# Loading a block an iteration before it is split, and two more weight tiles prepared ahead, in a fused attention and gated-MLP kernel

## The chip, the cores and the metric

The kernel runs on one core of one Trainium2 chip. The core has five engines with queues of their own: TensorE (PE, with its weight loads shown apart as PEld), VectorE (DVE), ScalarE (ACT), GpSimd (POOL) and SyncE (SP). SP and ACT also issue DMA transfers, which 16 DMA engines carry out. The metric is the device time of one execution in microseconds (us). Before the change the median of three runs is 1359.01 us (1357.99 to 1361.42).

## The reference

Linear attention over 8 batches, 8 heads, 576 positions and a head size of 64, and then a gated MLP on the 4608 tokens that come out, 512 wide, with 1536 hidden columns:

```python
def phi(x):
    proj = einsum('bhsd,df->bhsf', x, w_phi)             # 64 -> 128
    proj = proj - max(abs(proj), axis=-1, keepdims=True)
    return concatenate([exp(proj), exp(-proj)], -1)       # 256 features
q_p, k_p = phi(q), phi(k)
num = einsum('bhsf,bhfd->bhsd', q_p, einsum('bhsf,bhsd->bhfd', k_p, v))
den = einsum('bhsf,bhf->bhs', q_p, sum(k_p, axis=2)) + 1e-6
x = (num / den)                                           # to [4608, 512]
xn = x / sqrt(mean(x * x) + 1e-6) * rms_g
gate, val = xn @ w_gate, xn @ w_val                       # 512 -> 1536
out = (gate * sigmoid(gate) * val) @ w_out                # 1536 -> 512
```

## The kernel before

Every product is done at fp32 accuracy with a two-part form: an operand is split into a high part (a cast on ACT) and a low part (a subtraction on DVE or POOL), and three matmuls (high by high, low by high, high by low) stand for one. The helper that does a split is `_split`; its cast shows in the profile at L60 and its subtraction at L61. The moe weights arrive as 64-bit numbers, are decoded to fp32 by pieces and stored to DRAM (wgs, wvs, wos), to be loaded again where they are used.

There are three stages.

**Attention.** 8 batches with 4 pairs of heads give 32 pairs. A loop over `i` runs four parts of the work, front, mid, back and last, on four consecutive pairs, and merges their instructions into one stream. When the four pairs of a batch are done, the batch's x, transposed, lies in the DRAM tile xs. Whatever part of x is complete is used at once. Tokens come in 12 blocks of 384 (NB, T). Of the 12 column tiles of the hidden layer (128 columns each, NJ), the first three (J1) are computed during attention, from x that isn't normalised yet, because the norm is a factor for each token that can be multiplied in later. This work is called a fill. For each block a fill loads x (L461), splits it into xo (L60 and L61), and runs six units: three column tiles for gate (fg) and value (fv), 12 matmuls each (L476). Each result is copied on ACT from PSUM to a tile fo (L479, two buffers) and stored to gvs (L480). The weights of the fills, the pool wfp, stay in SBUF until the end of the next stage. The list `fills` holds load, split and units of the blocks that are complete, and from the moment it has more than 16 entries (RES) 2.5 entries are taken in each iteration. Two fills that need the last batch, for the blocks 10 and 11, are kept back (tail).

**Stage G** runs over the 12 blocks and, in each, over the nine other column tiles j (JN). `prep` loads a block's x (L141), sums its squares (ACT and POOL, then two matmuls with a matrix of ones), normalises x on DVE and splits it, with the low part on POOL. gv (L556) does 24 matmuls for a block and a j: gate to PSUM fp, value to gp. hidden applies Silu on ACT (L541), multiplies on DVE (L543) and stores h to hs in DRAM (L544). gv_raw loads the stored gvs of one of the first three column tiles (L563), multiplies the norm in and does the same. The gate and value weights come with block 0, by load_gv, which loads wc from ACT's own DMA queue (L536) and splits it to wg and wv. The two tail fills follow gv at block 0, j = 8 and block 1, j = 4.

**The output stage** multiplies hs by w_out for 18 groups (gi) of 256 tokens, with a Strassen-Winograd form of seven products in place of eight (L717, 18 matmuls each). Its weights are six pairs of tiles, wh and wl for kp = 0 to 5, made by load_o (L576): four transfers wc (L582), four subtractions on DVE (L583), two splits. Two of the six are made during stage G (PRE), four at the start of the output stage. A group's hidden values are loaded to a tile ht by hload (L688); from it, DVE makes the sums st (L652 to L660), and five operands are split with the low part on POOL, two (a11, a12) on DVE. hload for a group is written two groups ahead.

The order of the instructions on an engine isn't that of the program text. The Tile framework places them by a simulated timeline, an instruction where its operands and its buffer are ready by that simulation. Within an engine or queue the order is then fixed: an instruction that waits holds all behind it. Buffers of closed pools are given to new pools, and whoever takes one waits for its last user.

## Time and profile before

| | |
|---|---|
| median of three runs | 1359.01 us |
| the profiled execution's own time | 1366.07 us |
| its span on the core | 1364.3 us |
| mean granted TensorE clock | 0.977 of full |
| PE busy | 1303.9 us, 9108 matmuls |
| DVE, ACT, POOL busy | 878.0, 716.1, 610.6 us |
| HBM read, written | 126.04 MB, 69.50 MB |

In the profiled execution attention runs up to about 580 us, stage G from there to 1071 us, the output stage to the end. The lines below come from several views. A line of a timeline has the start (us from the span's beginning), the duration, engine, line, operation, tiles and count, and in brackets the idle time of that engine just before and what ended it. SPq and ACTq are the DMA issues of SP and ACT. A line of the waits says who waited for whom, the total, the number of times and the longest. A line of the groups has the busy time, the mean of one in ns, the idle time before and its releasers. "Granted clock" is the share of the full TensorE clock that was granted in a stretch.

### The profile page before, as it was taken

The numbers are of one execution on the slowest core, as the hardware profiler recorded it, in microseconds if no ns is written. First come the engines' busy times: TensorE is split into PE (matmuls) and PEld (weight loads), VectorE is DVE, ScalarE is ACT, GpSimd is POOL, SyncE is SP. The second block draws the span as 40 slices with busy tenths as digits, with TensorE's granted clock in tenths as the row PEclk, the third lists the DMA queues.
The fourth block names the chain that finished last, engine by engine and source line by source line (L and its number), as shares of the span: only waits on it lengthen the run. The fifth ranks groups of instructions, "written<-read, shape, count | busy, mean of one in ns | idle before, by whom it ended". The sixth has DMA issues, their size and how long they took to land.

```text
span 1364.3 us, 24782 instructions
## 1 busy us (share of the span) xinstructions
PE 1303.9 (96%) x9108; PEld 1291.0 (95%) x9108; DVE 878.0 (64%) x1293; ACT 716.1 (52%) x1490; POOL 610.6 (45%) x580
## 2 busy tenths in 40 slices
PE   7988989999999999989999999999999699999998
PEld 7888989999999999879999999999999699999998
DVE  6897857676778676453246665555542788787673
ACT  5986767776768676643333444333431344444441
POOL 3764635454646345501023333223311357776773
PEclk9997989998999999989999999999999899999999
DMA  5554555556545653475454544544433324534531
GB/s 153 129 141 113 151 166 151 156 152 181 172 144 156 174 158 112 140 216 156 150 180 159 170 130 159 156 148 131 132 125 109 99 97 144 166 125 147 159 128 48
DMA packets 198953, 197.18 MB, mean 145 GB/s; under 512 B 69104, under 2 KB 180848, under 8 KB 198832
## 3 DMA queue, kind: packets, MB, share of 16 engines
q1 hardware_dynamic: 189328, 190.88, 46.3%
q10 hardware_dynamic: 9504, 4.72, 1.2%
q8 instruction: 72, 1.18, 0.4%
q14 instruction: 49, 0.40, 0.1%
HBM read 126.04 MB, written 69.50 MB: 143 GB/s over the span
## 4 chain that ended last, share of the span: by engine, by line
PE 84%; DMA 5%; DVE 5%; ACT 2%; issue 2%; SPq 1%; ACTq 0%; POOL 0%; DVEq 0%
PE fp L556 16%; PE gp L556 16%; PE fp L476 8%; PE acc L346 7%; PE gz L717 5%; PE gd L717 5%; PE gy L717 5%; PE sm L410 3%; PE fp L717 3%; PE fp L410 3%; PE pp L306 2%; PE sm L293 2%; PE pp L308 2%; PE sm L359 2%; PE pp L307 2%
## 5 line engine op out<-in xcount | busy, mean ns | idle before, releaser
L375 POOL TENSOR_TENSOR ql<-eq,qh 128x256 fp32r<-128x256 f32 x256 | 218.8, 886 | 86.7 <-issue 50.2
L556 PE MATMUL fp<-xo,wg 128*128 128x384 f32 x1296 | 244.1, 336 | 6.4 <-ACT sl L541 6.4
L556 PE MATMUL gp<-xo,wv 128*128 128x384 f32 x1296 | 242.9, 335 | 0.0
L556 PEld LDWEIGHTS fp<-xo,wg 128*128 128x128 f32 x1296 | 228.1, 189 | 7.0 <-ACT sl L541 6.8
L556 PEld LDWEIGHTS gp<-xo,wv 128*128 128x128 f32 x1296 | 227.1, 188 | 0.0
L543 DVE TENSOR_TENSOR h<-sl,gp 128x384 f32<-128x384 f32 x108 | 59.6, 552 | 159.8 <-PE gp L556 112.1
L310 DVE TENSOR_REDUCE mx<-pp 128x4 f32<-128x512 f32 (+1 forms) x160 | 101.1, 633 | 69.4 <-PE pp L308 68.3
L541 ACT ACTIVATE sl<-fp 128x384 f32<-128x384 f32 x108 | 52.6, 488 | 177.2 <-PE fp L556 172.7
L346 PE MATMUL acc<-vm,ek 128*128 128x65 f32 x1024 | 134.8, 272 | 1.9 <-ACT ek L333 1.9
L346 PEld LDWEIGHTS acc<-vm,ek 128*128 128x128 f32 x1024 | 131.1, 197 | 2.2 <-ACT ek L333 2.2
L54 POOL TENSOR_TENSOR wa<-raw,wa 128x192 f32<-128x192 f32 (+1 forms) x112 | 62.4, 578 | 156.9 <-issue 85.4
L61 POOL TENSOR_TENSOR xo<-x,xo 128x768 fp32r<-128x768 f32 x24 | 52.3, 2202 | 160.1 <-ACT xo L60 160.1
L371 ACT ACTIVATE qh<-sm 128x512 fp32r<-128x512 f32 (+1 forms) x192 | 96.9, 505 | 0.0
L306 PE MATMUL pp<-wh,th 128*128 128x256 f32 x288 | 89.3, 310 | 6.4 <-ACT th L60 4.3
L476 PE MATMUL fp<-xo,fg 128*128 128x384 f32 x432 | 92.3, 348 | 1.9 <-ACT xo L60 1.8
L370 ACT ACTIVATE eq<-sm 128x512 f32<-128x512 f32 x128 | 78.3, 612 | 14.8 <-PE sm L359 14.0
L61 POOL TENSOR_TENSOR s2l<-st,s2h 128x768 fp32r<-128x768 f32 x18 | 35.0, 1947 | 112.7 <-ACT s2h L60 110.0
L308 PE MATMUL pp<-wh,tl 128*128 128x256 f32 x288 | 83.5, 298 | 0.0
L476 PE MATMUL fp<-xo,fv 128*128 128x384 f32 x360 | 80.6, 353 | 2.3 <-ACT fo L479 2.3
L307 PE MATMUL pp<-wl,th 128*128 128x256 f32 x288 | 82.3, 286 | 0.0
L377 POOL TENSOR_TENSOR ql<-eqr,qh 128x256 fp32r<-128x256 f32 x32 | 24.5, 765 | 124.9 <-ACT qh L371 119.5
L476 PEld LDWEIGHTS fp<-xo,fg 128*128 128x128 f32 x432 | 76.0, 192 | 2.9 <-ACT xo L60 2.1
(192 smaller groups left out, 3535.6 us busy)
## 6 DMA issues: line engine op xcount, KB each, us to landing
hs<-h SPq DMA_DIRECT2D x144, 192.0 KB
ht<-hs SPq DMA_DIRECT2D x18, 1536.0 KB
x<-xs SPq DMA_DIRECT2D x24, 768.0 KB
gvs<-fo SPq DMA_DIRECT2D x72, 192.0 KB
gvr<-gvs SPq DMA_DIRECT2D x36, 384.0 KB
rc<-di SPq DMA_DIRECT2D x32, 288.0 KB
kt<-in_k_dram SPq DMA_DIRECT2D x32, 256.0 KB
qt<-in_q_dram SPq DMA_DIRECT2D x32, 256.0 KB
```

The source lines that it names most:

```text
L61: (lo_eng or nc.vector).tensor_tensor(lo, x, hi.bitcast(F32), ALU.subtract)
L306: nc.tensor.matmul(o, th[:, cs], wh, start=True, stop=False)
L307: nc.tensor.matmul(o, th[:, cs], wl, start=False, stop=False)
L308: nc.tensor.matmul(o, tl[:, cs], wh, start=False, stop=True)
L310: nc.vector.tensor_reduce(mx[:, 0:2 * m], pp[:, 0:2 * m], axis=AX.X, op=ALU.max, apply_absolute_value=True)
L346: nc.tensor.matmul(acc[:, sg, h], e[h][:, sg, j], vm[:, h, j], start=False, stop=(h == 1 and j == T0 - 1))
L371: nc.scalar.activation(hi[:, sg], yi, AF.Exp, scale=1.0 - 2.0 * sg)
L375: nc.gpsimd.tensor_tensor(lo[:, sg, cs], ei[:, sg, cs], hi[:, sg, cs].bitcast(F32), ALU.subtract)
L410: nc.tensor.matmul(o[:, 0:SH], a[:, h, sg], e[:, sg, h, cs], start=(i == 0), stop=(i == 5))
L476: nc.tensor.matmul(fp, w, xx[x][:, c], start=(i == 0), stop=(i == 3 * NC - 1))
L556: nc.tensor.matmul(gp[:, 0:T], w, e[:, c], start=(i == 0), stop=(i == 3 * NC - 1))
L717: nc.tensor.matmul(place[n], a[:, kp], w[:, o], start=(first and kp == 0 and i == 0), stop=(kp == KP - 1 and i == 2), skip_group_check=True)
```

## The change

Loading x becomes a function of its own (fetch), called for fills by `load_x()` at the end of an iteration and followed by the split in a later iteration (`landed()`), so that the load stands one iteration ahead. The list of fills now holds block numbers, the list units only the matmul units; six of them are held back where 16 entries (units, loads and splits) were. The prep of block 0 goes into the same list three iterations earlier. fo has three buffers, which it shares with a small tile of prep. In stage G the loads for prep and for the tail fills stand some j ahead of their use as well, the second tail fill follows j = 6 of block 1 instead of j = 4, and gv_raw and the decoding change places.

The pool of the fill weights lies on the right side of SBUF and is closed after the last tail fill. Its place goes to the pool rg, which now holds four pairs of output weights (PRE = 4) made during stage G instead of two. With this the pools of the output stage are put in another order: the tiles that are there at the seam lie over others of stage G than before.

```diff
-    wfp = x_ctx.enter_context(tc.tile_pool(name="wfp", bufs=1))
+    wf_ctx = ExitStack()
+    wfp = wf_ctx.enter_context(tc.tile_pool(name="wfp", bufs=1, side="right"))
...
-    def prep(bk, pool, name):
-        bs = slice(bk * T, (bk + 1) * T)
+    def fetch(bk):
         x = xip.tile([128, NC, T], F32, name="x")
-        nc.sync.dma_start(out=x, in_=xsv[:, :, bs])
+        nc.sync.dma_start(out=x, in_=xsv[:, :, bk * T:(bk + 1) * T])
+        return x
+
+    def halves(x, lo_eng=None):
+        xhl = xop.tile([128, 2, NC, T], F32R, name="xo")
+        for c in range(0, NC, 2):
+            _split(nc, *(a[:, c:c + 2] for a in (xhl[:, 0], xhl[:, 1], x)), lo_eng=lo_eng)
+        return xhl[:, 0], xhl[:, 1]
+
+    def prep(x, pool, name):
...
-        sl = xm.tile([128, T], F32R, name="sl2", bufs=1)
+        sl = xm.tile([128, T], F32R, name="fo", bufs=3)
...
-                    (tail.append if b == B - 1 else fills.extend)(fill(blocks.pop(0)))
+                    (tail if b == B - 1 else fills).append(blocks.pop(0))
...
-            o = xm.tile([128, T], F32, name="fo", bufs=2)
+            o = xm.tile([128, T], F32, name="fo", bufs=3)
...
-    RES = 2 * (J1 * 2 + 2)
+    RES = J1 * 2
+    units, here = [], []
     dq = quota = 0.0
+    xb = {}
+
+    def load_x():
+        if fills and not here:
+            bk = fills.pop(0)
+            here.append((bk, fetch(bk or 0)))
+
+    def landed():
+        if here:
+            bk, x = here.pop(0)
+            if bk is None:
+                xb[0] = prep(x, ps_f, "fp")
+            else:
+                units.extend(fill(bk, *halves(x)))
...
-        if i == PR - 3:
-            nxt = prep(0, ps_f, "fp")
-        if len(fills) > RES:
-            quota += (NB - 2) * (J1 * 2 + 2) / PR
+
+        if i == PR - 6:
+            fills.insert(0, None)
+        if len(units) <= 3:
+            landed()
+        if len(units) + (len(fills) + len(here)) * J1 * 2 > RES:
+            quota += (NB - 2) * J1 * 2 / (PR - 5)
             nf = int(quota)
             quota -= nf
-            fl, fills[:] = fills[:nf], fills[nf:]
-            _merge([fl])
+            now, units[:] = units[:nf], units[nf:]
+            _merge([now])
+        load_x()
...
-    PRE = 2
+    PRE = 4
...
+            if j == 0 and bk + 1 < NB:
+                xn = fetch(bk + 1)
+            if bk + 1 < NB and j == (2 if bk == 1 else JN // 2):
+                xb[bk + 1] = prep(xn, ps_g, "gp")
+            if bk < 2 and j == (JN // 2, 2)[bk]:
+                xf = fetch(tail[0])
+            if bk < 2 and j == (JN - 1, 6)[bk]:
+                _merge([fill(tail.pop(0), *halves(xf))])
+                if not tail:
+                    wf_ctx.close()
+                    rg = ctx.enter_context(tc.tile_pool(name="rg", bufs=1, reuse_waits="tile", side="right"))
+            if j % (JN // J1) == 0:
                 gv_raw(bk, j // (JN // J1))
...
-    ohp = pool("ohp", bufs=2)
+    ohp = [pool("oh0")]
+    xof = pool("xof")
     ost = pool("ost", bufs=2)
-    xof = pool("xof")
-    xos = pool("xos")
-    xol = pool("xol")
-    xops = dict(a11=xof, a12=xof, s2=xof, s3=xof, s4=xol, a22=xol, s1=xos)
+    ohp.append(pool("oh1"))
+    ow = pool("ow", bufs=2)
     owc = pool("owc", bufs=2)
     owp = pool("owp")
-    ow = pool("ow", bufs=2)
+    xol = pool("xol")
+    xops = dict(a11=xof, a12=xof, s2=xol, s3=xol, s1=xol, s4=xol, a22=xol)
```

Three places show how the instructions move. A row has the line, the operation, the output tile, the inputs and the shape; numbers after a name tell its instances apart.

The first is SP's queue near the third block's load for a fill, at about 184 us of the profile before; x_3894 before is x_2936 after. Before:

```order
L236 DMA wgs_60<-wa_2541 128x384
L273 DMA rb_2917<-in_k_dram 128x1x64
L480 DMA gvs_58<-fo_2631 128x384
L480 DMA gvs_58<-fo_2647 128x384
L441 DMA xs_57<-nd_2195 128x576
L421 DMA di_2422<-dr_2420 128x9
L268 DMA kt_2913<-in_k_dram 128x2x256
L273 DMA rb_2917<-in_q_dram 128x1x64
L461 DMA x_3894<-xs_57 128x4x384
```

After:

```order
L424 DMA dr_2454<-dd_2455 128x9
L141 DMA x_2936<-xs_57 128x4x384
L37 DMA raw_2819<-in_moe_w_val_dram 128x768
L476 DMA gvs_58<-fo_2665 128x384
L476 DMA gvs_58<-fo_2681 128x384
L242 DMA wgs_60<-wa_2575 128x384
L274 DMA kt_2938<-in_k_dram 128x2x256
L279 DMA rb_2942<-in_k_dram 128x1x64
L279 DMA rb_2942<-in_q_dram 128x1x64
```

The load has moved ahead of the two gvs stores, the wgs store, kt and rb.

The second is ACT at the seam from attention to stage G, where the last copies of fo stand between loads (L536, after: L555) and casts of the first gate and value weights. Before:

```order
L479 COPY fo_8118<-fp_8105 128x384
L536 DMA wc_8245<-wgs_60 128x4x128
L536 DMA wc_8245<-wvs_61 128x4x128
L536 DMA wc_8291<-wgs_60 128x4x128
L479 COPY fo_8134<-fp_8121 128x384
L536 DMA wc_8291<-wvs_61 128x4x128
L60 CAST wg0_2_8172<-wc_8245 128x512
L60 CAST wv0_2_8174<-wc_8245 128x512
L60 CAST wg0_3_8176<-wc_8291 128x512
L60 CAST wv0_3_8178<-wc_8291 128x512
```

After:

```order
L475 COPY fo_8118<-fp_8105 128x384
L555 DMA wc_8290<-wgs_60 128x4x128
L555 DMA wc_8290<-wvs_61 128x4x128
L60 CAST wg0_2_8169<-wc_8252 128x512
L60 CAST wv0_2_8171<-wc_8252 128x512
L60 CAST wg0_3_8173<-wc_8290 128x512
L60 CAST wv0_3_8175<-wc_8290 128x512
L555 DMA wc_8328<-wgs_60 128x4x128
L475 COPY fo_8134<-fp_8121 128x384
L555 DMA wc_8328<-wvs_61 128x4x128
```

The last copy, fo_8134, has moved behind the second half of the wc load that it stood ahead of, the four casts, and the first half of the next load.

The third is SP's queue at the seam from stage G to the output stage (hs from h is a store of hidden values, ht from hs the load of a group, wc from wos a piece of output weights). Before:

```order
L544 DMA hs_59<-h_12767 128x384
L544 DMA hs_59<-h_12798 128x384
L582 DMA wc_12853<-wos_62 128x256 x4
L582 DMA wc_12869<-wos_62 128x256 x4
L688 DMA ht_13111<-hs_59 128x12x256
L582 DMA wc_12885<-wos_62 128x256 x4
L681 DMA out_0_dram<-ro_12943 128x512 x2
```

After:

```order
L563 DMA hs_59<-h_12800 128x384
L601 DMA wc_12869<-wos_62 128x256 x2
L563 DMA hs_59<-h_12831 128x384
L601 DMA wc_12869<-wos_62 128x256 x2
L713 DMA ht_12901<-hs_59 128x12x256
L713 DMA ht_12903<-hs_59 128x12x256
L601 DMA wc_12885<-wos_62 128x256 x4
L713 DMA ht_13111<-hs_59 128x12x256
L706 DMA out_0_dram<-ro_12943 128x512 x2
```

Of the weight pieces here, those of the kernel before that are left are the pairs 4 and 5 (wc_12869 and wc_12885). The loads ht_12901 and ht_12903 of the first two groups, which stood some 220 rows further up, in the middle of stage G, now stand here, behind the last store of hidden values.

More of the change, by code (lines that the diff above doesn't have):

```diff
@@ L454, with fill @@
     blocks = list(range(NB))
-    def fill(bk):
-        xx = {}
-        def fetch():
-            xx["x"] = xip.tile([128, NC, T], F32, name="x")
-            nc.sync.dma_start(out=xx["x"], in_=xsv[:, :, bk * T:(bk + 1) * T])
-        def split():
-            xhl = xop.tile([128, 2, NC, T], F32R, name="xo")
-            xx["h"], xx["l"] = xhl[:, 0], xhl[:, 1]
-            for c in range(0, NC, 2):
-                _split(nc, *(a[:, c:c + 2] for a in (xx["h"], xx["l"], xx["x"])))
+    def fill(bk, xh, xl):
+        xx = dict(h=xh, l=xl)
         def unit(j, wi):
```

24 lines of the change are left out of this document (9 added, 15 removed).

## The prediction

> **What bounds the kernel now.** I read the page's busy shares and chain first, then the busy time by stretches, then the waits and timelines around each stretch in which TensorE (PE) is not full.
>
> ```profile
> PE 1303.9 (96%) x9108; PEld 1291.0 (95%) x9108; DVE 878.0 (64%) x1293; ACT 716.1 (52%) x1490; POOL 610.6 (45%) x580
> DVE  6897857676778676453246665555542788787673
> PE 84%; DMA 5%; DVE 5%; ACT 2%; issue 2%; SPq 1%; ACTq 0%; POOL 0%; DVEq 0%
> ```
>
> PE is busy for 1303.9 us of a span of 1364.3 us, and it is 84% of the chain that ended last (DVE's row is its busy tenths in 40 slices of the span). The change issues the same matmuls, so it can only touch the 60.4 us in which PE idles and the time in which PE runs at less than its full clock after such idling. Both show in the stretches (columns: window, length, then busy us and instructions of PE, weight load, DVE, ACT, POOL, then granted clock, DMA share, GB/s):
>
> ```profile
> 190.00:200.00 10.00, 6.38 (x25) 6.09 (x26) 4.21 (x6) 8.60 (x23) 3.58 (x5) 0.66 0.33 85
> 320.00:330.00 10.00, 8.08 (x48) 7.74 (x48) 6.21 (x9) 7.00 (x17) 2.25 (x3) 0.78 0.36 123
> 470.00:480.00 10.00, 7.66 (x45) 7.54 (x46) 7.13 (x12) 9.04 (x21) 4.21 (x7) 0.83 0.41 113
> 580.00:600.00 20.00, 13.55 (x67) 13.04 (x67) 8.22 (x14) 7.60 (x13) 0.00 (x0) 0.84 0.85 239
> 1070.00:1080.00 10.00, 5.60 (x25) 4.58 (x24) 8.58 (x6) 6.67 (x9) 6.23 (x3) 0.82 0.23 74
> 1080.00:1100.00 20.00, 12.29 (x58) 10.50 (x57) 17.92 (x22) 6.33 (x8) 5.00 (x3) 0.66 0.42 131
> 1100.00:1120.00 20.00, 20.00 (x172) 20.00 (x171) 16.63 (x15) 9.17 (x14) 14.21 (x7) 1.00 0.31 103
> ```
>
> I price a stall as the idle time plus busy time times (1 − clock). At 190 to 200 us that is 3.6 + 6.4 × 0.34 = 5.8 us. The two seams are the dear ones: 580 to 600 us costs 6.4 + 13.55 × 0.16 = 8.6 us, and 1070 to 1100 us costs 12.1 + 1.0 + 4.2 = 17.3 us.
>
> **Part 1: x fetched an iteration ahead (attention stage).** The four longest waits of an ACT cast for a fill's x, with other work of ACT queued behind:
>
> ```profile
> 108.96 1.57 ACT L60 CAST xo<-x 128x768 fp32r<-128x768 f32 x2 [3.59 <-DMA x<-xs]
> 191.40 1.56 ACT L60 CAST xo<-x 128x768 fp32r<-128x768 f32 x2 [5.97 <-DMA x<-xs]
> 322.90 1.56 ACT L60 CAST xo<-x 128x768 fp32r<-128x768 f32 x2 [4.87 <-DMA x<-xs]
> 470.32 1.56 ACT L60 CAST xo<-x 128x768 fp32r<-128x768 f32 x2 [5.08 <-DMA x<-xs]
> 193.50 0.58 PE L306 MATMUL pp<-wh,th 128*128 128x256 f32 x1 [4.07 <-ACT th L60]
> 325.05 1.55 PE L346 MATMUL acc<-vm,ek 128*128 128x65 f32 x8 [1.92 <-ACT ek L333]
> 472.34 1.11 PE L359 MATMUL sm<-ident,yq 128*128 128x128 f32 x4 [2.61 <-ACT nd L412]
> 183.91 0.41 SPq L461 DMA_DIRECT2D x<-xs  x1
> ```
>
> The second x was issued at 183.91 and its cast began at 191.40, so a fetch takes about 7.5 us from issue to use; the casts that PE waited for (th, ek, nd) stand behind xo on ACT. If every such stall went, it would be worth, with the rows above, 5.8 (at 190), 1.9 + 8.08 × 0.22 = 3.7 (at 320) and 2.3 + 7.66 × 0.17 = 3.6 us (at 470). But the new order does not remove them all. Up to about 158 us the two programs have the same order on each engine, so the first stall stays. For the second (third block's x), the load now stands ahead of six others (two gvs stores, the wgs store, kt and two rb) that stood ahead of it before, and three more ACT instructions separate it from its cast: I take that stall as gone, −5 us. For the rest I count the ACT instructions from the last one whose result a store ahead of the load waits for to the cast. At the stall of 322.9 this count goes from 6 to 7, so it stays. At 470.3 it goes from 7 to 14, and at the next fill from 16 to 5: I take that as a swap, at nothing. The split is still put where x is expected, not where it surely is. The only buffer for x is still one, so a fetch still waits for the previous split. Bounds: −13 (all three later stalls gone) to +3 (the second stays, one more of about 3.6 us). Chosen: **−5**.
>
> **Part 2: the third buffer for fo and the seam to stage G.** Around 575 to 597 us ACT copies fill results to fo, and each copy waits until an older fo has left:
>
> ```profile
> 576.97 3.25 PE L476 MATMUL fp<-xo,fv 128*128 128x384 f32 x12 [2.27 <-ACT fo L479]
> 584.57 0.48 ACT L479 COPY fo<-fp 128x384 f32<-128x384 f32 x1 [6.23 <-DMA gvs<-fo]
> 591.59 0.62 ACT L60 CAST wg<-wc 128x512 fp32r<-128x512 f32 x1 [2.87 <-DMA wc<-wgs]
> 597.57 6.48 PE L556 MATMUL fp<-xo,wg 128*128 128x384 f32 x24 [6.45 <-ACT sl L541]
> ```
>
> The copy at 584.57 idled ACT for 6.23 us, and behind it stood the load of a wc half, then the casts of wg and wv, then the loads and casts of the next pair, and at their end the Silu for which PE waited 6.45 us. With three fo buffers that copy waits for PE alone, and it now stands behind one more load, four casts and the first half of the next load. The weight loads have their own pace (the cast at 591.59 waited 2.87 us for one, at a DMA share of 0.85), so not all 6.23 us comes back; I take half, **−3**, with 0 (transfers set the pace) and −8.6 − 2.3 = −11 (seam gone) as bounds; −6 is the most that the copy's own wait pays for.
>
> **Part 3: tail fills in stage G.** Before, the first one's x was issued after the split of the next block on POOL:
>
> ```profile
> 610.13 0.33 PE L152 MATMUL gp<-sq,ones 128*128 128x384 f32 x1
> 610.48 2.24 PE L556 MATMUL fp<-xo,wg 128*128 128x384 f32 x12
> 612.55 2.24 PE L556 MATMUL gp<-xo,wv 128*128 128x384 f32 x12
> 617.41 3.65 POOL L61 TENSOR_TENSOR xo<-x,xo 128x768 fp32r<-128x768 f32 x2 [48.34 <-ACT xo L60]
> 622.78 0.39 SPq L461 DMA_DIRECT2D x<-xs  x1
> 628.23 1.56 ACT L60 CAST xo<-x 128x768 fp32r<-128x768 f32 x2 [5.33 <-DMA x<-xs]
> 629.11 0.52 PE L476 MATMUL fp<-xo,fg 128*128 128x384 f32 x1 [1.83 <-ACT xo L60]
> ```
>
> From the ones-matmul to the end of POOL's split is 621.06 − 610.13 = 10.9 us, the fetch 5.45, the first cast 0.8: 17.2 us. The first tail fill now has its fetch ahead, so I take −1 of its 1.83 us stall. The second (block 1) now has 96 matmuls between the ones-matmul and itself; at 12 in 2.07 us (610.48 to 612.55) that is 16.6 us, 0.6 us short of 17.2, and I take +1.5 with a slow clock behind it. Sum **+0.5**, from −2 to +3.5.
>
> **Part 4: the seam to the output stage.** The end of the last gv matmul, the weight work after it, and the next stage:
>
> ```profile
> 1069.08 2.25 PE L556 MATMUL gp<-xo,wv 128*128 128x384 f32 x12
> 1072.87 14.34 SPq L582 DMA_DIRECT2D wc<-wos  x8
> 1092.53 1.74 SPq L582 DMA_DIRECT2D wc<-wos  x4
> PE fp L717 <- DVE a11l L61: 3.1, 1, 3.1
> 1106.46 2.12 PE fp L717 x18
> 1060.56 0.95 DVE L652 TENSOR_TENSOR st<-ht 128x768 f32<-128x768 f32 x1
> ```
>
> Group 0 of the output stage ends at 1106.46 (group 1 starts there), 35.1 us after gv ended at 1071.33. Its 126 matmuls at 20 / 172 = 0.116 us are 14.7 us, so 20.4 us is lost. The four tile pairs kp 2 to 5 set that: their loads are issued from 1072.87 to 1094. The operands were ready early: DVE read ht at 1060.56. The change takes two of the four tile pairs out of the seam (they are prepared in stage G beside a full PE, on a DVE whose slices there read 2 to 6 tenths; uncovered, it would cost what it saves here, at most half of the 20.4 us). Eight transfers of 128 KB, four splits and eight subtractions go from the seam. But the first ht tile moves the other way. Its buffer oh0 now lies over x's buffers, and its load, which stood far back in stage G, now stands right behind the last hs store, which waits for the last multiplication on DVE. So it is issued about 2 us after gv ends. What it takes from there is in the steady stage:
>
> ```profile
> 1142.74 0.38 SPq L688 DMA_DIRECT2D ht<-hs  x1
> 1150.87 2.31 DVE L652 TENSOR_TENSOR st<-ht 128x768 f32<-128x768 f32 x1 [1.43 <-DMA ht<-hs]
> L61 POOL TENSOR_TENSOR a22l<-ht,a22h 128x768 fp32r<-128x768 f32 x18 | 44.7, 2482 | 0.7 <-ACT a22h L60 0.7
> 1073.89 2.57 DVE L61 TENSOR_TENSOR a11l<-ht,a11h 128x768 fp32r<-128x768 f32 x1
> ```
>
> From 1142.74 to 1150.87 is 8.1 us, so ht lands 10 to 11.5 us after gv, and PE idles for about 11 us. Then everything that was done ahead before follows it: a cast, two splits and four additions on DVE, five splits of some 2.2 us (11 us) on POOL, and the last weight pair, whose load stands behind both ht loads on SP's queue. I put group 0's end 23 to 28 us after the landing: 33 to 39.5 us after gv, against 35.1. Chosen 36, **+1**, from −3 to +5. The prices of both halves nearly cancel.
>
> On the clock, the row of 1080 to 1100 us (0.66) follows several gaps of 0.2 to 3.1 us. The Trainium skill, "TensorE: Matmul & The Clock Gate", Part 1, says that the clock is halved after an idle window of about 3.4 us and released after as long a busy one. By that rule the one long gap of the change would cost a single ramp of some 1.7 us (estimate from that page) where I allow up to 5. The trace disagrees in part: no gap before 1100 us was over 3.1 us, and the clock fell all the same.
>
> **The sum.** −5 − 3 + 0.5 + 1 = −6.5 us on the profiled execution's own 1366.07 us (span 1364.3), which lies 7.06 us above the median 1359.01. The stalls are likely no smaller in a median run in their sum, though I cannot see it, so I take the same difference there: 1359.01 − 6.5 = 1352.5, rounded to **1353**.
>
> **Rivals.** (A) *No change*: the second stall of part 1 comes back in another place, because the cast is still put where the transfer is expected, and the seam to G keeps its weight transfers' pace. Then −1 − 1 + 0.5 + 1: about 1358.5. For it speaks the group of all those casts:
>
> ```profile
> L60 ACT CAST xo<-x 128x768 fp32r<-128x768 f32 x48 | 38.9, 838 | 58.9 <-DMA x<-xs 31.7 <-DVE x L158 21.3 <-PE gp L476 5.8
> ```
>
> Of its 58.9 us of idle time 31.7 us is for the transfer of x, and the four waits above make 19.5 us of that: 12.2 us lies in waits that cost PE little so far, and a moved order can make them cost. Against: the copy of fo alone held ACT for 6.23 us. (B) *Slower*: the late ht decides. If the two ht loads, issued one behind the other, share the engines, ht lands after two times 8.1 us, 18 us after gv, and with 28 us behind it group 0 ends 46 us after, +11 us; its second group, whose ht came no sooner, starts some 2 us short: +13. With the gains −7.5 the time is 1364.5. It decides (slower by 0.3%) from where group 0 ends some 47 us after gv with full gains, or 43 us with half of them. The Trainium skill, "DMA: Bandwidth & Descriptors", "Queues, rings and completion order", speaks against it: descriptors of one ring are consumed in order, so the first load would not share with the second. No row of before shows two such loads together. (C) *Much faster*: all three later x stalls go (−13), the seam to G gives 6, the output seam −3: 1359 − 22 + 0.5 = 1337.5; half of that, 1345, is where I put it.
>
> **Chances.** Forecast 0.45 (its own range 1349 to 1357), A 0.22, B 0.20, C 0.13. About 0.3%, 4.1 us, can be told from no change, so faster is below 1354.9 and slower above 1363.1. Of the forecast 0.33 is faster, 0.11 the same and 0.01 slower; of A 0.20 is the same and 0.02 faster; of B 0.15 is slower and 0.05 the same; C is faster. That gives faster 0.48, same 0.36, slower 0.16. The range, 1343 to 1365, takes in A, most of B and half of C.
>
> **What would show it.** Right, if the changed profile has no ACT cast of xo waiting about 6 us for x near 190 us while the wait near 109 us stays; if the last fo copy before the first Silu of stage G waits for PE; if PE idles near 11 us in one piece after the last gv matmul, released by a cast of a11 or by ht; and if group 1 starts 33 to 40 us after it. Wrong, if new casts of xo wait 3 us or more for x elsewhere with PE idle behind them (A), if ht lands over 14 us after the last gv matmul (B), or if PE's wait for the first Silu is under 2 us and no attention window is below a clock of 0.9 (C).

## The result and the profile after

The changed kernel takes 1375.74 us (median of four runs, 1373.57 to 1381.36) where the kernel before, run beside it, takes 1360.22 us (four runs, 1357.99 to 1363.72). The ratio is 1.0118, 95% interval 1.0079 to 1.0157: it is slower by 1.2%, above the predicted range. The profiled execution took 1376.67 us (span 1374.9), 10.6 us more than the profiled one before, which was itself long for its kernel: 5.9 us above the median.

The page of the changed kernel, busy times and the chain that ended last, by engine and by line:

```profile
PE 1300.6 (95%) x9108; PEld 1284.4 (93%) x9108; DVE 880.2 (64%) x1293; ACT 713.3 (52%) x1490; POOL 605.5 (44%) x580
PE 65%; DMA 14%; DVE 12%; issue 3%; ACT 2%; POOL 2%; SPq 1%; ACTq 0%; DVEq 0%; POOLq 0%
PE fp L575 9%; PE gp L575 9%; PE fp L472 7%; PE gd L742 5%; PE gy L742 5%; PE gz L742 5%; PE acc L352 5%; DMA x<-xs 5%; DMA gvr<-gvs 3%; PE sm L416 3%; PE fp L742 3%; PE fp L416 2%; PE pp L314 2%; PE pp L312 2%; PE pp L313 2%
```

PE is busy no longer than before, but its part of the chain fell from 84% to 65%. Transfers hold 14% (5% before) and DVE 12% (5% before) in its place, and two of the transfers have names of stage G's loads: x from xs, and gvr from gvs.

Where the time went is read from stretches, with the price of the prediction (idle time of PE, plus busy time times one minus granted clock). Three stretches of stage G, from the kernel before and then from the changed one (columns as in the prediction):

```profile
660.00:760.00 100.00, 100.00 (x579) 100.00 (x578) 49.93 (x76) 39.88 (x72) 21.94 (x23) 1.00 0.51 167
760.00:860.00 100.00, 100.00 (x579) 100.00 (x578) 55.37 (x89) 38.47 (x77) 33.64 (x34) 1.00 0.48 156
860.00:960.00 100.00, 100.00 (x579) 100.00 (x578) 52.14 (x86) 40.50 (x77) 31.60 (x32) 1.00 0.47 149
```

```profile
660.00:760.00 100.00, 99.90 (x576) 99.58 (x576) 42.62 (x68) 34.47 (x64) 17.93 (x20) 1.00 0.40 136
760.00:860.00 100.00, 92.88 (x511) 90.86 (x510) 55.30 (x84) 36.48 (x73) 29.52 (x33) 0.97 0.45 149
860.00:960.00 100.00, 95.03 (x532) 93.35 (x531) 53.72 (x88) 38.97 (x71) 23.53 (x27) 0.98 0.44 144
```

Before, stage G had a full PE at full clock from 660 us to its end. Now PE issues 511 and 532 matmuls in the second and third stretch where it issued 579. Summed in steps of 10 us over the whole of each profile, the prices are these (us; the last column but one is the price of the 60 us behind the end of the last gv matmul; the last column is no price but the whole time from that end to the end of the span):

| | attention, to 570 | seam A to G, 570 to 605 | tail fills, 605 to 660 | stage G, from 660 | seam G to O | output stage |
|---|---|---|---|---|---|---|
| before | 44.1 | 12.1 | 3.2 | 0.0 | 17.1 | 293.0 |
| after | 41.2 | 10.5 | 6.1 | 16.4 | 18.4 | 287.3 |
| attention part alone (b_att) | 40.0 | 8.8 | 4.5 | 0.0 | 18.1 | 293.6 |
| after, gv_raw and decoding put back (g_raw) | 38.0 | 5.9 | 0.9 | 0.0 | 18.6 | 287.2 |

The stages differ by −2.8, −1.6, +2.9 and +16.4 us, 14.9 in all; the last gv matmul ends 16.3 us later (1087.62 against 1071.33), and the output stage gives 5.7 us back: +10.6 us, the whole difference of the two spans. One profile of a kernel doesn't fix the smaller of these numbers: b_raw below, whose attention stage is the one of the kernel before, instruction for instruction on PE, has 39.6 us in the first column where that kernel has 44.1.

What PE waited for shows in the changed kernel's waits (the second row is of the seam to the output stage) and, below, in the seven rows of its PE timeline from 660 us to the end of stage G that have a wait:

```profile
PE fp L575 <- ACT sl L560: 14.5, 7, 3.6
PE fp L742 <- DVE wl L61: 4.2, 1, 4.2
```

```profile
771.17 2.38 PE L575 MATMUL fp<-xo,wg 128*128 128x384 f32 x12 [1.24 <-ACT sl L560]
805.47 2.35 PE L575 MATMUL fp<-xo,wg 128*128 128x384 f32 x12 [0.32 <-ACT sl L560]
812.90 3.09 PE L575 MATMUL fp<-xo,wg 128*128 128x384 f32 x12 [3.00 <-ACT sl L560]
855.71 3.70 PE L575 MATMUL fp<-xo,wg 128*128 128x384 f32 x12 [2.44 <-ACT sl L560]
896.10 2.37 PE L575 MATMUL fp<-xo,wg 128*128 128x384 f32 x12 [0.56 <-ACT sl L560]
916.44 2.38 PE L575 MATMUL gp<-xo,wv 128*128 128x384 f32 x12 [0.98 <-DVE h L562]
939.12 3.03 PE L575 MATMUL fp<-xo,wg 128*128 128x384 f32 x12 [3.32 <-ACT sl L560]
```

They sum to 11.9 us; a slow clock behind them makes the rest of 16.4. The dear four come about every 42 us, or twice that; 42 us is the time of a block. One of them in the timelines of the queue, ACT and DVE:

```profile
804.92 0.49 ACT L560 ACTIVATE sl<-fp 128x384 f32<-128x384 f32 x1 [2.46 <-DVE h L562]
805.72 0.40 SPq L141 DMA_DIRECT2D x<-xs  x1
806.22 0.60 SPq L582 DMA_DIRECT2D gvr<-gvs  x1
811.54 0.52 ACT L152 ACTIVATE ss<-x 128x384 f32<-128x384 f32 x1 [5.47 <-DMA x<-xs]
812.38 0.47 ACT L560 ACTIVATE sl<-fp 128x384 f32<-128x384 f32 x1
812.55 0.96 DVE L583 TENSOR_TENSOR gvr<-gvr,ri 128x768 f32<-128x768 f32 x1 [4.12 <-DMA gvr<-gvs]
814.58 0.54 DVE L562 TENSOR_TENSOR h<-sl,gp 128x384 f32<-128x384 f32 x1
```

ACT starts a Silu 2.46 us late, because DVE has not finished an h. Then the loads of x (768 KB) and gvr (384 KB) are issued one behind the other. ACT stands 5.47 us before the Square of x, with the next Silu behind it, and DVE 4.12 us before the multiplication of gvr, with the next h behind that. PE needs that Silu, and idles 3.00 us. The groups of those operations (busy, mean ns | idle before, and for whom), of the kernel before and then of the changed one:

```profile
L541 ACT ACTIVATE sl<-fp 128x384 f32<-128x384 f32 x108 | 52.6, 488 | 177.2 <-PE fp L556 172.7 <-DVE h L543 2.8 <-DVE wp L51 1.7
L564 DVE TENSOR_TENSOR gvr<-gvr,ri 128x768 f32<-128x768 f32 x36 | 39.5, 1098 | 26.6 <-DMA gvr<-gvs 26.5
L143 ACT ACTIVATE ss<-x 128x384 f32<-128x384 f32 x12 | 6.4, 530 | 38.2 <-DMA x<-xs 38.2
```

```profile
L560 ACT ACTIVATE sl<-fp 128x384 f32<-128x384 f32 x108 | 52.6, 487 | 153.1 <-PE fp L575 126.2 <-DVE h L562 26.2 <-issue 0.6
L583 DVE TENSOR_TENSOR gvr<-gvr,ri 128x768 f32<-128x768 f32 x36 | 38.0, 1056 | 72.7 <-DMA gvr<-gvs 72.7
L152 ACT ACTIVATE ss<-x 128x384 f32<-128x384 f32 x12 | 6.3, 529 | 51.5 <-DMA x<-xs 51.5
```

DVE's wait for gvr grew from 26.5 to 72.7 us, ACT's for DVE's h from 2.8 to 26.2, ACT's for x from 38.2 to 51.5. Which part of the change does this, and which wait is the cause, the profile alone doesn't say.

### The profile page after: what moved, and what is told of

Same layout as the page of the kernel before. It is cut to its first block, busy times and chain, and to the rows that moved or that the text cites. A ratio compares the mean times of both kernels' runs of the same rounds, so it can differ in the third digit from the quotient of the medians.

```text
span 1374.9 us, 24771 instructions
## 1 busy us (share of the span) xinstructions
PE 1300.6 (95%) x9108; PEld 1284.4 (93%) x9108; DVE 880.2 (64%) x1293; ACT 713.3 (52%) x1490; POOL 605.5 (44%) x580
## 4 chain that ended last, share of the span: by engine, by line
PE 65%; DMA 14%; DVE 12%; issue 3%; ACT 2%; POOL 2%; SPq 1%; ACTq 0%; DVEq 0%; POOLq 0%
PE fp L575 9%; PE gp L575 9%; PE fp L472 7%; PE gd L742 5%; PE gy L742 5%; PE gz L742 5%; PE acc L352 5%; DMA x<-xs 5%; DMA gvr<-gvs 3%; PE sm L416 3%; PE fp L742 3%; PE fp L416 2%; PE pp L314 2%; PE pp L312 2%; PE pp L313 2%
## 5 line engine op out<-in xcount | busy, mean ns | idle before, releaser
L575 PE MATMUL fp<-xo,wg 128*128 128x384 f32 x1296 | 247.4, 339 | 14.7 <-ACT sl L560 14.5
L575 PE MATMUL gp<-xo,wv 128*128 128x384 f32 x1296 | 246.6, 338 | 6.3 <-DVE wv L61 5.2
L575 PEld LDWEIGHTS gp<-xo,wv 128*128 128x128 f32 x1296 | 230.3, 191 | 7.3 <-DVE wv L61 5.6
L61 POOL TENSOR_TENSOR xo<-x,xo 128x768 fp32r<-128x768 f32 x24 | 44.6, 1878 | 190.7 <-ACT xo L60 190.7
L376 ACT ACTIVATE eq<-sm 128x512 f32<-128x512 f32 x128 | 78.1, 610 | 17.3 <-PE sm L365 16.8
L583 DVE TENSOR_TENSOR gvr<-gvr,ri 128x768 f32<-128x768 f32 x36 | 38.0, 1056 | 72.7 <-DMA gvr<-gvs 72.7
L472 PE MATMUL fp<-xo,fv 128*128 128x384 f32 x360 | 77.1, 346 | 0.7 <-ACT nd L418 0.7
```

The costliest lines, as they stand in the source:

```text
L376: nc.scalar.activation(ei[:, sg], yi, AF.Exp, scale=1.0 - 2.0 * sg)
L472: nc.tensor.matmul(fp, w, xx[x][:, c], start=(i == 0), stop=(i == 3 * NC - 1))
L575: nc.tensor.matmul(gp[:, 0:T], w, e[:, c], start=(i == 0), stop=(i == 3 * NC - 1))
```

## The experiments

Each kernel was run beside the kernel before, whose median was 1359.33, 1361.14, 1359.57 and 1359.61 us in the four sets. Ratios are to it, with 95% intervals. "Price" and "costs" of a stage are as in the table above.

### Which part of the change

Two theories stood at first. W: the two added weight pairs, now made in stage G, load its engines. Q: the new order, with gv_raw at j = 0, 3, 6 and the decoding at 1, 4, 7, where before it was the other way about.

**g_raw**, the changed kernel with both put back:

```diff
-            if j % (JN // J1) == 0:
+            if j % (JN // J1) == 1:
                 gv_raw(bk, j // (JN // J1))
-            if bk > 1 and j % (JN // J1) == 1 and decs:
+            if bk > 1 and j % (JN // J1) == 0 and decs:
```

> The changed kernel with one part of its stage G undone: gv_raw follows j = 1, 4, 7 and the decoding j = 0, 3, 6 again. The load of x then stands six rows ahead of the next gvr load on SP, and on ACT the order around the first Square of a block's x is that of the kernel before. Theory Q (the 16.4 us that stage G lost come from the order in which x, gvr, Square and Silu follow each other once gv_raw was moved): the stage's stalls go, the time is 14 to 17 us below the changed kernel, about 1360. Theory W (the two more pairs of output weights made in stage G load its queues and DVE): at most 3 us less than the changed kernel.

1352.24 us (ten runs), ratio 0.9951 (0.9925 to 0.9978). Stage G's price is 0.0 again, with four weight pairs still made in it. That is theory Q, though the time is 23.5 us below the changed kernel where 14 to 17 were expected: the tail fills and the seam to stage G are cheaper too (0.9 and 5.9 us, where they were 6.1 and 10.5). The group of the multiplication in this kernel:

```profile
L583 DVE TENSOR_TENSOR gvr<-gvr,ri 128x768 f32<-128x768 f32 x36 | 37.6, 1045 | 21.8 <-DMA gvr<-gvs 21.6
```

**g_pre2**, the changed kernel with two weight pairs made in stage G in place of four:

```diff
-    PRE = 4
+    PRE = 2
```

> The changed kernel with two pairs of output weights made in stage G, not four (PRE = 2); the order in stage G is the same up to the third pair. Theories Q1 and Q2: the stage G stalls between 760 and 910 us stay, the one at 916 us may go: 0 to 3 us less in stage G, and 4 to 10 us more at the seam to the output stage, where four pairs must be made behind a late ht. Theory W: 8 us or more less in stage G.

1389.03 us, ratio 1.0197 (1.0155 to 1.0240). Stage G still costs 11.7 us, 4.7 less than with four pairs: more than the 3 us that Q left room for, and short of the 8 that W asked for. With g_raw, which has all four pairs and no loss, W falls as the cause. The seam to the output stage costs 27.3 us in place of 18.4: group 0 ends 43.6 us after the last gv matmul, where it was 34.2. So the two added pairs are worth about 9 us at the seam: with the late ht of the new layout and only two pairs ready, the seam is nearly as long as in the slower rival of the prediction (46 us).

**b_raw**, the kernel before with nothing but the two places exchanged:

```diff
-            if j % (JN // J1) == 1:
+            if j % (JN // J1) == 0:
                 gv_raw(bk, j // (JN // J1))
...
-            if bk > 1 and j % (JN // J1) == 0 and decs:
+            if bk > 1 and j % (JN // J1) == 1 and decs:
```

> The kernel before with nothing but gv_raw moved to j = 0, 3, 6 and the decoding to j = 1, 4, 7. If that move alone makes the stalls of stage G: the kernel before gains them too, 10 to 17 us more, 1371 to 1378, with the Silu's wait for DVE near 26 us. If it takes the move together with the earlier load of x or with four pairs of weights: under 4 us more.

1375.72 us, ratio 1.0107 (1.0080 to 1.0134), stage G 9.5 us, the tail fills 6.4 us (3.2 before), and the waits of its gvr group are like those after the change:

```profile
L564 DVE TENSOR_TENSOR gvr<-gvr,ri 128x768 f32<-128x768 f32 x36 | 34.5, 958 | 62.6 <-DMA gvr<-gvs 62.3
```

The exchange alone makes the kernel before as slow as the whole change does, and undoing it makes the changed kernel faster than before. That settles which part it is.

**b_att**, the kernel before with the attention part alone (fetch, halves, the lists of fills, fo with three buffers); stage G and the output stage stay as they were, and there each fetch stands at its split:

```diff
-                _merge([tail.pop(0)])
+                t = tail.pop(0)
+                _merge([fill(t, *halves(fetch(t)))])
...
-                xb[bk + 1] = prep(bk + 1, ps_g, "gp")
+                xb[bk + 1] = prep(fetch(bk + 1), ps_g, "gp")
```

> Only the first part of the change: x of a fill loaded an iteration ahead, three fo buffers, the new quota and the earlier prep of block 0; stages G and O are those of the kernel before, with PRE = 2 and the old pools. My prediction's terms for this part: -5 (attention) and -3 (seam to stage G), so about 1352; what the changed kernel's trace showed of it: -2.9 and -1.6, so about 1356. If the gain there is only a shift of stalls: within 2 us of before.

1356.79 us (ten runs), ratio 0.9975 (0.9951 to 1.0000): a small gain, with an interval that reaches to none. Its stages are in the table above.

### Which half of the exchange

**raw_only** puts back gv_raw alone (j = 1, 4, 7, the decoding at the same j), **dec_only** the decoding alone (both at j = 0, 3, 6).

```diff
-            if j % (JN // J1) == 0:
+            if j % (JN // J1) == 1:
```

> The changed kernel with gv_raw back at j = 1, 4, 7, while the decoding stays at j = 1, 4, 7, so that both fall on the same j. If the place of gv_raw alone makes the stalls of stage G: they go, about 1352 as with both undone. If gv_raw and decoding must only be apart: the stalls stay or grow, 1365 or more.

1356.10 us, ratio 0.9978 (0.9957 to 0.9999). Stage G costs 1.1 us.

```diff
-            if bk > 1 and j % (JN // J1) == 1 and decs:
+            if bk > 1 and j % (JN // J1) == 0 and decs:
```

> The changed kernel with the decoding back at j = 0, 3, 6, while gv_raw stays at j = 0, 3, 6. If the decoding next to prep (both at j = 4) makes the stalls: they go, about 1352 to 1356. If gv_raw beside the load of x at j = 0 makes them: they stay, 1370 or more.

1360.95 us, ratio 1.0013 (0.9983 to 1.0042). Stage G costs 4.7 us. The groups of gvr and of the Square, in the kernel with gv_raw put back and then in the one with the decoding put back:

```profile
L583 DVE TENSOR_TENSOR gvr<-gvr,ri 128x768 f32<-128x768 f32 x36 | 40.3, 1119 | 9.7 <-DMA gvr<-gvs 9.2
L152 ACT ACTIVATE ss<-x 128x384 f32<-128x384 f32 x12 | 6.4, 531 | 52.3 <-DMA x<-xs 52.3
```

```profile
L583 DVE TENSOR_TENSOR gvr<-gvr,ri 128x768 f32<-128x768 f32 x36 | 37.0, 1027 | 44.9 <-DMA gvr<-gvs 44.5
L152 ACT ACTIVATE ss<-x 128x384 f32<-128x384 f32 x12 | 6.4, 530 | 60.9 <-DMA x<-xs 60.9
```

Either half takes back most of the 16.4 us, so neither place alone costs much (4.7 us that of gv_raw, 1.1 that of the decoding); the loss takes both. dec_only's time lies between the two that were expected of it. The wait for gvr goes with the price of the stage (9.2 us with 1.1, 44.5 with 4.7, 72.7 with 16.4); the wait for x does not.

**dec_127** moves a third of the decoding only, from j = 4 to j = 2. Theory D puts the loss down to the decoding's place (prep stands at j = 4 too), theory G to the transfer of gvr, before which DVE waits.

```diff
-            if bk > 1 and j % (JN // J1) == 1 and decs:
+            if bk > 1 and j in (1, 2, 7) and decs:
```

> The changed kernel with the decoding of a stage G block at j = 1, 2 and 7, where it has j = 1, 4 and 7: it no longer falls on j = 4, where prep's normalisation keeps DVE and its split keeps POOL busy; gv_raw stays at j = 0, 3, 6. Theory D (two waits in a row use up the slack of the two PSUM banks: the Silu's wait for DVE, 26.2 us in all, which comes from normalisation and decoding behind one another, and then the Square's wait for x): the Silu's wait for DVE falls under 10 us, and stage G loses under 6 us where it lost 16.4; time 1357 to 1365. Theory G (DVE's wait for the gvr load, 72.7 us, makes the stalls): no more than 4 us less, 1371 or more.

1373.31 us, ratio 1.0098 (1.0067 to 1.0129). Stage G costs 13.4 us, DVE waits 71.7 us for gvr, and the Silu's wait for DVE's h is 17.3 us where D asked for less than 10: D falls, G stands.

### Which transfer

**g_fetch** loads a block's x at its prep and no longer at j = 0, so that gvr's load at j = 0 has no x in front of it:

```diff
-            if j == 0 and bk + 1 < NB:
-                xn = fetch(bk + 1)
...
-                xb[bk + 1] = prep(xn, ps_g, "gp")
+                xb[bk + 1] = prep(fetch(bk + 1), ps_g, "gp")
```

> The changed kernel with x of a stage G block loaded where prep uses it (j = 4, or 2), not at j = 0; gv_raw stays moved. The gvr load now stands ahead of the x load on SP, and one more Silu stands ahead of the first Square on ACT. Theory Q1 (the Square, waiting on ACT for x, holds the Silu that frees a PSUM bank): the wait of the Square stays near 4 to 5 us but holds no Silu that PE needs; at least 10 of the 16.4 us go. Theory Q2 (gvr, behind x on the ring, holds DVE): DVE's wait for gvr falls from 72.7 us to under 45 and the stalls go too; what remains tells the two apart, since a remaining PE stall behind a Square speaks for Q1 alone. Theory W: no change over 3 us.

1372.11 us, ratio 1.0090 (1.0062 to 1.0119). Stage G costs 13.9 us and DVE waits 59.4 us for gvr. The small gain is neither theory's number, but it says that x's load in front of gvr's is not what makes most of gvr's wait.

What does can be read from the timelines of SP and DVE, load by load from 660 us on. The loads are no slower, but for nine that are issued right behind an x: where DVE waited, the multiplication began 4.1 us after the issue of its load in the kernel before, and in the changed kernel 3.6 us after it, or 5.8 us for those nine. What changed is how soon DVE comes to the multiplication and stands: on average 3.3 us after the load's issue in the kernel before, 3.4 in g_raw and 4.5 in raw_only, but 2.8 in dec_only, and about 2 in the changed kernel, in b_raw, in g_fetch and in dec_127, the four whose stage G costs 9.5 us or more.

**x2buf** gives every second block's x a buffer of its own, to take the Square's wait away (with PRE = 3, to make room):

```diff
-    def fetch(bk):
-        x = xip.tile([128, NC, T], F32, name="x")
+    def fetch(bk, p=None):
+        x = (p or xip).tile([128, NC, T], F32, name="x")
...
+    xip2 = g_ctx.enter_context(tc.tile_pool(name="xip2", bufs=1))
...
-    PRE = 4
+    PRE = 3
...
-                xn = fetch(bk + 1)
+                xn = fetch(bk + 1, xip2 if bk % 2 else None)
```

> The changed kernel with a second buffer for the x of stage G's blocks (every other block has its own), so that x is loaded a block before its Square; room is made with PRE = 3 in place of 4. gv_raw and decoding stay moved. Theory Q1 (five of the seven stalls come from the Square that waits on ACT for x, ahead of a Silu): the wait of the Square falls from 51.5 us to under 10, the stalls of about 3 us at 813, 856 and 939 us go, stage G loses 3 to 6 us where it lost 16.4. Theory D (DVE is what is late: norm, decoding and gvr one behind the other hold the multiplication that frees the Silu's buffer): the Silu's waits for DVE (26.2 us) stay, and at least 9 of the 16.4 us stay with them. The output stage is some 2 us longer by PRE = 3 either way.

1382.27 us, ratio 1.0170 (1.0131 to 1.0210). It tells nothing of the theory: the framework moved the Square forward with the load, so it waited 49.2 us as ever. Stage G costs 11.6 us; the third pair's absence shows at the seam (25.5 us in place of 18.4).

**no_gvr** loads gvr in blocks 0 and 1 only and works on the kept tile after that, with a minimum in place of the multiplication. So it leaves out the right hidden values of the first three column tiles from block 2 on; the instructions of the engines stay, but for their order, which the framework sets anew.

```diff
-        r = wk.tile([128, 2, T], F32, name="gvr", bufs=1)
-        nc.sync.dma_start(out=r, in_=gvv[j][:, :, bk * T:(bk + 1) * T])
-        nc.vector.tensor_tensor(r, r, xb[bk][2].unsqueeze(1).broadcast_to([128, 2, T]), ALU.mult)
+        if bk < 2:
+            r = wk.tile([128, 2, T], F32, name="gvr", bufs=1)
+            nc.sync.dma_start(out=r, in_=gvv[j][:, :, bk * T:(bk + 1) * T])
+            kept["r"] = r
+        r = kept["r"]
+        nc.vector.tensor_tensor(r, r, xb[bk][2].unsqueeze(1).broadcast_to([128, 2, T]), ALU.mult if bk < 2 else ALU.min)
```

> The changed kernel without the loads of gvr from block 2 on: the multiplication on DVE takes the last loaded tile (as a minimum, so that values stay bounded), so the results of the first three column tiles are left out there, and no wait for that transfer is left. Theory G (DVE, held by gvr's transfer, holds the multiplication that stores h and frees the Silu's buffer): stage G loses under 5 us where it lost 16.4. Theory Q1 (the Square's wait for x): 10 us or more stay.

**no_x** doesn't load x for blocks 4 to 11; prep normalises the same tile once more, so the hidden values of these blocks are not those of their tokens.

```diff
-            if j == 0 and bk + 1 < NB:
+            if j == 0 and bk + 1 < NB and bk < 3:
```

> The changed kernel without the loads of x for blocks 4 to 11: prep normalises the tile that is there once more, so these blocks' x is left out, and the Square waits for no transfer; gvr is loaded as before. Theory Q1: stage G loses under 5 us where it lost 16.4. Theory G: 10 us or more stay. If both runs lose little, it takes the two waits one behind the other.

Without gvr's load: 1359.32 us, ratio 0.9991 (0.9954 to 1.0028), stage G 0.3 us. Without x's: 1382.66 us, ratio 1.0146 (1.0084 to 1.0208), stage G 25.8 us. The groups of the kernel without gvr's loads, and of that without x's:

```profile
L588 DVE TENSOR_TENSOR gvr<-gvr,ri 128x768 f32<-128x768 f32 x36 | 35.6, 988 | 8.4 <-DMA gvr<-gvs 7.5
L152 ACT ACTIVATE ss<-x 128x384 f32<-128x384 f32 x12 | 6.4, 532 | 51.6 <-DMA x<-xs 51.6
```

```profile
L583 DVE TENSOR_TENSOR gvr<-gvr,ri 128x768 f32<-128x768 f32 x36 | 34.4, 956 | 77.0 <-DMA gvr<-gvs 76.9
L152 ACT ACTIVATE ss<-x 128x384 f32<-128x384 f32 x12 | 6.4, 531 | 52.8 <-DVE x L167 38.3 <-DMA x<-xs 14.5
```

With gvr's transfers gone, the Square's wait of 51.6 us stays and costs PE nothing. With most of x's transfers gone the loss stays and grows. So DVE's wait for gvr is what the loss needs, and x's transfer is not. The Square still waited 52.8 us in the run without x's loads, now mostly for DVE. Whether the gvr wait would cost as much with no wait before the Square stays open: no kernel here had the first without the second. Why the loss grew to 25.8 us without x's loads was not tested either; there DVE comes to the multiplication only 1.5 us after the load's issue.

### What the seam to the output stage is worth

These start from g_raw. **seam** keeps xo's pool through the output stage and loads the first two ht there, during the last block, so that they no longer lie over x's buffer:

```diff
+    xop = ctx.enter_context(tc.tile_pool(name="xop", bufs=3))
...
-    xop = x_ctx.enter_context(tc.tile_pool(name="xop", bufs=3))
...
+            if bk == NB - 1 and j in (3, 6):
+                hload(j // 3 - 1)
...
-        h = ohp[gi % 2].tile([128, NJ, 256], F32, name="ht")
+        h = xop.tile([128, NJ, 256], F32, name="xo")
...
-    hload(0)
-    hload(1)
```

> The changed kernel with gv_raw and decoding back in place, and with the first two loads of the output stage early: ht takes the buffers of xo (three of 12 KB), whose oldest is free a block before the end, and its first two loads are written into the last block, at j = 3 and j = 6. The 9.6 us wait of PE for a11h should go. If the late ht is what sets this seam, group 0 ends 22 to 27 us after the last gv matmul, not 34, and the time is 1341 to 1347. If the last two pairs of output weights set it as well, it ends after 29 to 33 us and the time is 1348 to 1352.

1344.47 us (six runs), ratio 0.9899 (0.9866 to 0.9932). PE goes from the last gv matmul into the output stage without a stop, group 0 ends 25.6 us after it (34.2 after the change), and the 60 us from there cost 10.1 us in place of the 18.6 of g_raw.

**seam2** adds two more buffers for weight pieces, so that the last pair's load isn't behind the third ht:

```diff
-    owc = pool("owc", bufs=2)
+    owc = pool("owc", bufs=4)
```

> The kernel with the early first loads of the output stage, and four buffers in place of two for the pieces of its last two weight pairs, so that the last pair's pieces are loaded ahead of the third group's ht and not behind it. If that pair now sets the seam: group 0 ends 20 to 23 us after the last gv matmul, where it took 25.6, and the time is 2 to 5 us less. If DVE's and POOL's splits of group 0 set it: within 1 us.

1343.61 us, ratio 0.9870 (0.9841 to 0.9898). Group 0 ends at 24.9 us, 0.7 sooner: the load's place in the queue was not what was left of that seam.

**seam_r** also moves the last two weight pairs to the right side of SBUF:

```diff
-    owp = pool("owp")
+    owp = ctx.enter_context(tc.tile_pool(name="owp", bufs=1, reuse_waits="tile", side="right"))
```

> The same with the last two weight pairs on the right side of SBUF too, right below the other four (143328 to 172000 bytes in a partition). In all kernels so far a matmul of the output stage takes 113.3 ns where its weight tile lies on the right and 116 to 120 ns where it lies on the left. If the side decides: the last two pairs fall to 113.3 ns and the stage's 2268 matmuls take 3 us less. If it is the place above 172000 bytes, or the earlier making of the tile: they stay at 116 to 119 ns. The tiles lie over ones that stage G uses to its end, so the seam may be 1 to 5 us longer.

1341.10 us (1331.66 to 1344.84), ratio 0.9848 (0.9805 to 0.9891). It is the best kernel of this case, 1.5% under the kernel before. Its lead over seam2 is inside the intervals; what the side does is read from the pace of the matmuls, in the last section.

## Why the prediction was wrong

**The step that failed is one that isn't there.** The part-by-part sum, −5 − 3 + 0.5 + 1, went from attention over the seam and the tail fills to the output stage, and had no term for "gv_raw and the decoding change places", though the change's text has those words. Stage G was priced only for its tail fills, and the DVE load of the two added weight pairs was rightly called covered, by the full PE. The same full PE hid the exchange from the reasoning. Its cover ran out: an exchange that adds no instruction made DVE stand before a transfer for 46 us more (26.5 to 72.7) and cost 16.4 us of stage G; without that, the other terms as measured leave a gain. With the exchange undone the change gives 1352.24 us, where 1353 was forecast for the whole. That agreement is in part luck: some 5 us of the gain are from the output stage behind the seam, which had no term.

All that the prediction named as signs of being right came (no wait of 6 us near 190 us, the last fo copy that waits for no store, PE's idle piece behind gv, the start of group 1), and the time was still slower: none of the signs looked at stage G.

What could have been seen blind is that the wait for gvr was in the profile before: 26.5 us in 25 waits, in front of a multiplication with the next h behind it, at no cost. A moved step whose wait is covered needs its own line in the sum: what covers it, by how much, and in which order it now stands with what follows.

**Part 1, attention** (−5 predicted, from −13 to +3): −2.8 us here, −4.1 in b_att, −6.1 in g_raw. The size isn't shown by these: b_raw, with the old attention stage, reads −4.5 too. The waits of a cast for x, from the changed kernel's ACT timeline, and a row of its PE waits:

```profile
105.91 1.57 ACT L60 CAST xo<-x 128x768 fp32r<-128x768 f32 x2 [1.97 <-DMA x<-xs]
173.81 0.83 ACT L60 CAST xo<-x 128x768 fp32r<-128x768 f32 x1 [4.75 <-DMA x<-xs]
185.32 1.57 ACT L60 CAST xo<-x 128x768 fp32r<-128x768 f32 x2 [1.06 <-DMA x<-xs]
318.30 1.56 ACT L60 CAST xo<-x 128x768 fp32r<-128x768 f32 x2 [3.80 <-DMA x<-xs]
485.57 1.58 ACT L60 CAST xo<-x 128x768 fp32r<-128x768 f32 x2 [2.08 <-DMA x<-xs]
PE sm L416 <- ACT nd L418: 3.0, 2, 2.7
```

The first stays at a smaller size, the one near 190 falls from 5.97 to 1.06 us, the one near 322 stays, and that at 470 has gone, with a lesser one at 485. But the fill ahead, whose cast waited 0.63 us at 176.63 before, now waits 4.75 us, and PE idles 2.2 us in three pieces in the 7 us after it: a part of the wait only moved, which was the sign of rival A. From 160 to 200 us the price still fell as forecast, from 7.3 us (7.5 in b_raw) to 3.8 (4.2 in b_att, 2.3 in g_raw).

Another stall had no term. From 450 to 480 us the three kernels with the new attention stage lose 7.1, 6.8 and 5.2 us, where the kernel before and b_raw lose 3.9 and 1.1. The normalisation of block 0's x, which DVE began at 425.32 us before, begins at 450.66 us in the changed kernel; an nd on ACT behind it waits for DVE, and PE 2.7 us for that nd. No run separates this from the rest of the part.

**Part 2, seam to stage G** (−3, from −11 to 0): −1.6 us here, −3.3 in b_att, −6.2 in g_raw. The copy was read rightly, by the changed kernel's ACT and PE rows there, but not what it is worth:

```profile
581.08 0.47 ACT L475 COPY fo<-fp 128x384 f32<-128x384 f32 x1
591.79 3.69 PE L575 MATMUL fp<-xo,wg 128*128 128x384 f32 x12 [3.64 <-ACT sl L560]
573.14 4.21 PE L575 MATMUL gp<-xo,wv 128*128 128x384 f32 x12 [5.24 <-DVE wv L61]
```

The last copy waits for no store, and PE's wait for the first Silu fell from 6.45 to 3.64 us. (In b_raw, with two fo buffers, it was 4.44 us, so not all of that fall is the copy's.) But 5.24 us now stand before a gv matmul that waits for its split weights: the weights' own pace, the bound of that part. PE's two waits here sum to 8.9 us, where those before, 2.27 and 6.45, sum to 8.7; some 2 us of the 5.24 lie before 570 us, and so in the attention column. A gain at this seam is not shown for the changed kernel.

**Part 3, tail fills** (+0.5, up to +3.5): +2.9. The first tail fill was to lose 1 us of its stall of 1.83; it waits 3.00 us now, in the changed kernel's PE timeline. That too goes with the exchange: in b_raw, which doesn't have the earlier fetch, it waits 3.13 us, and in g_raw, which has it without the exchange, 0.47 us, where the tail fills cost 2.3 us less than before.

```profile
624.05 0.69 PE L472 MATMUL fp<-xo,fg 128*128 128x384 f32 x1 [3.00 <-ACT xo L60]
```

**Part 4, seam to the output stage** (+1; group 0's end 33 to 39.5 us after gv): −0.9, at 34.2 us against 35.1. The changed kernel's PE and SP rows:

```profile
1089.68 1.27 SPq L713 DMA_DIRECT2D ht<-hs  x2
1096.38 0.83 ACT L60 CAST a11h<-ht 128x768 fp32r<-128x768 f32 x1 [2.44 <-DMA ht<-hs]
1097.26 0.58 PE L742 MATMUL fp<-wh,a11h 128*128 128x256 f32 x1 [9.64 <-ACT a11h L60]
```

ht is issued 2.1 us after gv and is there 6.7 us later (8.1 predicted); PE idles 9.64 us in one piece (about 11 predicted), released by a11. So the two halves of this part do nearly cancel: the two added pairs are worth about 9 us by g_pre2, and the late ht costs about 8.5 us by seam, which took it away (18.6 to 10.1 us). The two ht loads did not share the engines in a way that held the first up, so rival B's mechanism didn't come. The Trainium skill, "DMA: Bandwidth & Descriptors", "Queues, rings and completion order", says that descriptors of one ring are consumed in order, which spoke against it; the trace agrees with that: 6.7 us from the issue to the first ht's use, with the second right behind it on the queue.

On the clock, the changed kernel's stretches behind that gap and around a stall of stage G:

```profile
800.00:820.00 20.00, 16.69 (x86) 15.95 (x85) 13.31 (x22) 9.39 (x21) 9.81 (x10) 0.91 0.48 156
1087.00:1107.00 20.00, 8.94 (x51) 7.63 (x49) 14.79 (x14) 7.21 (x9) 8.24 (x4) 0.74 0.65 207
1107.00:1127.00 20.00, 16.52 (x126) 16.52 (x127) 17.15 (x19) 8.77 (x12) 11.58 (x6) 0.83 0.25 80
```

The slow clock behind the gap cost 8.94 × 0.26 + 16.52 × 0.17 = 5.1 us, with the second gap of 4.2 us before a weight split in it: about the 5 us allowed for. In the stretch of stage G the clock is 0.91 though no gap there is over 3.00 us. The Trainium skill, "TensorE: Matmul & The Clock Gate", Part 1, puts the idle window that halves the clock at about 3.4 us; here, as in the kernel before (0.66 from 1080 to 1100 us, with no gap over 3.1 us), shorter gaps were enough. Behind the last gv matmul, an estimate from that page's figures for the two gaps over that window is 3.4 us (two ramps of 1.7 us), against the 5.1 us of the rows.

**Sizes of the rivals.** Rival B had slower for the seam, and the seam was no slower. That the time came out slower is no support for B. The chance of slower, 0.16, hung on that one place but for 0.01.

**What no term had.** The output stage behind the seam runs 4.8 us shorter (5.7 less the 0.9 of group 0's end). Its matmuls are as many as before; they follow one another faster.

## What to carry to other kernels

When a change moves a step that reads a transfer, price the step itself even where the engine that bounds the kernel is full around it: take its wait from the groups before, name what stands behind it on its engine, ask how soon after the load's issue the engine will now come to it, and how much more wait the cover bears. A table of losses by stage from both profiles, with the same price in each, finds the stage at once, and undoing the moved step alone in the new kernel and making it alone in the old one settles it from both sides. A tile that is needed at a seam should not lie over one that is in use up to the seam: giving the first two ht a place of their own was worth about as much here (1352.24 to 1344.47 us) as all of the change without its loss.

## What the runs showed of the hardware that was not expected

The pace of the output stage's fp32 matmuls, whose 128x256 operand is a weight tile in SBUF, went with the place of that tile. In the output stage the mean time from one matmul's start to the next, worked out from the starts in the trace and sorted by weight pair 0 to 5, is 119.3, 113.7, 116.2, 119.5, 118.0 and 120.0 ns before, where pairs 0 and 1 lie on the right side of SBUF and the others on the left, and 117.7, 113.5, 113.3, 113.3, 116.2 and 119.3 ns after, where pairs 0 to 3 lie on the right. Pair 0 follows the last pair of the product ahead. In seam_r, with all six on the right side, each is at 113.3 to 113.6 ns. One row of 20 us with a full PE at full clock shows it in the number of matmuls; the kernel before, then the changed one and seam_r:

```profile
1200.00:1220.00 20.00, 20.00 (x172) 20.00 (x172) 14.85 (x15) 8.35 (x11) 13.23 (x7) 1.00 0.59 184
```

```profile
1200.00:1220.00 20.00, 20.00 (x175) 20.00 (x174) 16.43 (x17) 8.25 (x11) 13.90 (x7) 1.00 0.52 157
```

```profile
1200.00:1220.00 20.00, 20.00 (x179) 20.00 (x178) 18.36 (x16) 8.45 (x11) 16.35 (x8) 1.00 0.54 161
```

They hold 172, 175 and 179 matmuls. From seam2 to seam_r only the side of the pool changed, and the output stage went from 277.6 to 275.5 us, though the 60 us at its start cost 1.6 us more. Why the place matters is open: no run separated the side from the addresses, or from what else lies and is written there.
